# VectorE's small steps moved to PSUM, ScalarE and GpSimd, one lo piece, and one scale per weight matrix

## The chip, the core and the metric

The kernel runs on one NeuronCore of a Trainium2 chip. Its time is the device time of one execution in microseconds (us), the median of several runs. The engines are TensorE (PE, matmuls; PEld loads its weights), VectorE (DVE), ScalarE (ACT), GpSimd (POOL) and SyncE (SP), which only issues DMAs. [...]

## The reference

An attention over 8 batches, 12 heads, 448 tokens and head size 64 is followed by a layer that mixes each token with the one before it:

```python
q_n, k_n = rmsnorm(q, g_q), rmsnorm(k, g_k)        # x / sqrt(mean(x*x) + 1e-6) * g
scores = q_n @ k_n.T / 8; attn = softmax(scores)
x = (attn @ v)                                      # heads joined: 8 x 448 x 768
x_prev = x shifted by one token (zero in front)
xk = mu_k * x + (1 - mu_k) * x_prev
xr = mu_r * x + (1 - mu_r) * x_prev
k = relu(xk @ w_k)                                  # 768 x 1024
out = sigmoid(xr @ w_r) * ((k * k) @ w_v)           # 768 x 768, 1024 x 768
```

All inputs are fp32 apart from the three weight matrices, which arrive as 64-bit floats; the kernel reads each of their values as two 32-bit words and makes fp32 of them.

## The kernel before, in words

All products that matter are computed to about fp32 from fp16: each operand is split into hi (its fp16 value) and lo (the rest, again fp16), and a product is three matmuls, hi x hi, hi x lo and lo x hi. The first three of 24 quads (a quad is four heads of a batch, so three quads are a batch) use fp32 operands instead.

**Attention.** `stats` squares a quad's q and k (ScalarE), folds the halves (GpSimd), sums (VectorE) and takes the inverse root of 28 numbers per partition in `rsqrt`: two steps that make a first guess and three Newton rounds of three VectorE steps. With the two steps that scale and add epsilon that is 13 small VectorE steps, all on SBUF tiles (sst, stm, ss). `preps` scales q and k and splits and transposes them. `scores` computes a group, 128 query rows of two heads against 448 keys, in two PSUM banks; there are seven groups in a quad, 168 in all. `expo` takes the row maximum (VectorE, tile sums) and the exponential (ScalarE, in place in PSUM). In `split` ScalarE writes hi, scaled by 1 / sum, to SBUF (tile nat), and VectorE writes lo in two pieces of 64 and 384 columns (lines 889 and 890), so that lo's 64-token blocks stand rotated by one; a DMA transpose on SP's queue turns hi and lo for the second product. `attends` multiplies with v; `PASSES` lists which block goes with which block of v.

**v.** `vload` brings one pair of heads into one of two vf tiles, `vprep` squares it for a bound, takes a power of two as its scale (tile bstat), writes hi (ScalarE, vh) and lo (VectorE, vl). `batch_scales` works out a batch's scales (tile bsc, VectorE).

**Mixture.** `mix` (lines 952 to 967), twelve times per batch (six d for xk and six for xr): GpSimd multiplies the shifted x into df, VectorE adds the product of x to it, ScalarE writes hi, GpSimd lo.

**Weights.** w_k, w_r and w_v are cut in 20 tiles of 128 columns (8, 6 and 6; 768 or 1024 values per partition). `wload` loads each in two halves, issued on ScalarE's queue; `weights` turns each half from 64-bit words to fp32 in a wf tile: GpSimd the low part, ScalarE the top part into a PSUM bank of the `mm` share, VectorE joins the two. `wsplit` (1014 to 1038) then takes for each tile a scale from the diagonal of its Gram product (a TensorE product, VectorE's dg, a product with ones, VectorE's maximum, two small VectorE steps on WSC) and splits the tile into hi and lo (`wkh`, `wkl` and so on): tiles 1 to 13 on GpSimd with a ScalarE copy, the others on ScalarE and VectorE.

**Second layer.** `moe` runs batch by batch: eight products for k (144 matmuls), then, after `until(lambda: st["wdone"] == NW)` in the first batch, products of 128 tokens with w_r and w_v (294 matmuls per batch on average), each in a PSUM bank of the `mm` share. `gate` runs three tanh per 384 columns, one per weight tile, `store` multiplies, and GpSimd scales 384 columns before the output DMA on SP.

**What sets the order.** Every step is a Python generator that yields instructions; `Plan.run` emits, engine by engine, the instruction that could start first by the kernel's own price list (`price`), less 0.1 ns per unit of its thread's priority. The order on each engine and DMA queue is fixed when the program is built, and semaphores alone keep it at run time. The weights' priority is

```python
PRIO_W + (BOOST_W if st["want"] == "w" else 0) + (plan.now() - W_START - W_GAP * st["wdone"]) * W_PUSH
```

with W_GAP = 10e3 ns: it rises with time and falls by one step with each tile that is done. PSUM banks are lent by shares: `Share(psum, most, spare)` gives at most `most` banks and only while more than `spare` are free: scores (5, 1), second layer (2, 0), values and others (2, 0). A score group asks for two free banks, three in the first quads.

Since one helper records all instructions, every row of the profile has line 273; the tile names tell the steps apart (a name with x at its end is the same kind of tile added late).

Of the kernel before, what the change touches and what calls it, by code (L numbers as in the profile page):

```python
# [31 lines left out]
WF_BUFS = 2  # L32
# [6 lines left out]
LOW_TILES = range(0, 20)  # L39
POOL_TILES = range(1, 14)  # L40
# [36 lines left out]
Q_DVE = 1  # L77
PE_T = 6
# [10 lines left out]
WB_A = 'ot'  # L89
WB_B = 'mm'  # L90
# [5 lines left out]
W_GAP = 10e3  # L96
# [7 lines left out]
LATE_BUFS = (("kf", 1), ("df", 1), ("nat", 1))  # L104
# [65 lines left out]

def price(op):
# [4 lines left out]
    ps = any(in_psum(x) for x in aa)  # L176
    if e == "DVE":
        two = "in1" in kw
        c = n / 0.96 + (128 if two and n > 64 else 64)
        return c, c + 80  # L180
    if e == "ACT":
        c = n * 0.868 + (127 if ps else 67)
        if kw.get("accum_out") is not None:
            return c + 52, c + 170
        return c, c + 110
    if op.fn.__name__ == "memset":
        return 50, 95
    if "in1" in kw:
        c = n * (2.15 if kw["out"].dtype == F16 else 2.0) + 40
    elif n < 100:  # L190
        c = n * 0.868 + 180
    else:
        c = n * 1.27 + 35
    return c, c + 45

# [10 lines left out]
class Plan:  # L206
# [60 lines left out]
    def emit(self, ops):  # L267
# [18 lines left out]
        elif ops[0].fn.__name__.startswith("dma"):  # L286
# [3 lines left out]
            if "transpose" in op.fn.__name__:  # L290
                w, iss, tot = n / 128 * 1.21, 1600, 4000
            else:
                w, iss, tot = n / 55, 640, 3300
# [12 lines left out]
        else:  # L306
# [7 lines left out]
            if e == "POOL" or e == "DVE" and not any(in_psum(x) for x in op.kw.values() if isinstance(x, bass.AP)) and width(op.kw["out"]) > 2:  # L314
# [126 lines left out]
def attn_moe_kernel(tc, q, k, v, g_q, g_k, mu_k, mu_r, w_k, w_v, w_r, out):  # L441
# [15 lines left out]
    banks = {n: Share(psum, *c) for n, c in (("sc", SC_SHARE), ("mm", MM_SHARE), ("ot", OT_SHARE))}  # L457
# [18 lines left out]
    for nm, kt, n in (("wk", ND, D_FF), ("wr", ND, D_MODEL), ("wv", NF, D_MODEL)):  # L476
        WS[nm] = (wpool.tile([P, kt, n], F16, name=nm + "h"), wpool.tile([P, kt, n], F16, name=nm + "l"))
    pairs = [(b, hp) for b in range(B) for hp in range(NP)]
    quads = [(b, j) for b in range(B) for j in range(NP // 2)]
    NQ, NPAIR, NSS, NSL = len(quads), len(pairs), 4 * NT, (NT + 1) // 2  # L480
    VFREE = [const.tile([P, 2 * NSL, HD], F32, name="vf%d" % n) for n in range(VF_BUFS)]
# [5 lines left out]

    def WB(ci):
        return WB_A if ci < NF else WB_B

# [9 lines left out]
    def late():  # L500
# [11 lines left out]
        "vh": Ring(ap_, [P, 2 * NSL, HD], F16, "vh", VH_BUFS, plan),  # L512
# [9 lines left out]
        "raw": Ring(stage, [P, NF // 2, 2 * P], I32, "raw", RAW_BUFS, plan),  # L522
# [4 lines left out]
    for name, plan_ in (("kk", KK_LENT), ("xk", XK_LENT)):  # L527
# [5 lines left out]
        for n in plan_:  # L533
# [10 lines left out]
            if len(r.shape) == 3:  # L544
# [27 lines left out]
    def mu_stats():  # L572
        yield from until(lambda: st["lu"] >= 1 and len(WFT))
# [34 lines left out]
    def stats():  # L608
        for u in range(NQ):
# [4 lines left out]
            tm = small.tile([P, NSS], F32, name="stm", bufs=3)  # L614
# [11 lines left out]
            yield V.tensor_scalar(out=ss[:, 0:2 * NT], in0=ss[:, 0:2 * NT], scalar1=1.0 / HD, scalar2=1e-6, op0=ALU.mult, op1=ALU.add)  # L626
            yield V.tensor_scalar(out=ss[:, 2 * NT:NSS], in0=ss[:, 2 * NT:NSS], scalar1=gm[:, 3:4], scalar2=gm[:, 4:5], op0=ALU.mult, op1=ALU.add)
            yield from rsqrt(V, y, ss, tm, NEWTON_ON == "POOL" and G_)
# [69 lines left out]
    def vload():  # L698
        yield from until(lambda: st.get("vf") and st.get("lu", 0) >= LEAD_V)
        for i in range(NPAIR):  # L700
# [3 lines left out]
            yield SP.dma_start(out=vf.rearrange("p a c -> p (a c)"), in_=v[i])  # L704
# [15 lines left out]
    def vprep(js):  # L720
# [7 lines left out]
        for e, i in enumerate(js):  # L728
            yield from until(lambda: i in VF and st["tq"] >= GATE_V)
            vf = VF.pop(i)  # L730
            if half:
                vh = yield from R["vh"].get()
                vl = yield from R["vl"].get()
                sq = vh.bitcast(BF16)
# [4 lines left out]
            yield A.activation(out=sq, in_=vf, func=AF.Square, accum_out=vs[:, e:e + 1])  # L739
# [7 lines left out]
        yield V.tensor_reduce(out=vs[:, 2:2 + n], in_=pt[:, 0:n * P].rearrange("p (a c) -> p a c", c=P), axis=AX.X, op=ALU.max)  # L747
        banks["ot"].put(pt)
        sv, iv = s_[:, hp:hp + n], s_[:, NP + hp:NP + hp + n]
        yield V.tensor_scalar(out=sv.bitcast(I32), in0=vs[:, 2:2 + n].bitcast(I32), scalar1=24, scalar2=23, op0=ALU.logical_shift_right, op1=ALU.logical_shift_left)  # L750
# [487 lines left out]
```

## Time and profile before

| | |
|---|---|
| runs (us) | 1014.79, 1018.15, 1019.3; median 1018.15 |
| the profiled execution | 1015.21 us, of which span 1013.4 |
| mean granted TensorE clock | 0.961 of full speed |
| busy, share of the span | PE 926.0 (91%), DVE 812.7 (80%), ACT 746.0 (74%), POOL 691.8 (68%) |
| HBM read / written | 51.98 MB / 11.01 MB |
| DMA, mean over the span | 146 GB/s |

Matmuls overlap in the records, so 91% for PE is the time in which at least one of them was in flight. A row of the groups reads: line, engine, operation, out<-in by tile names, shapes, count | busy us, mean ns of one | idle time of the engine in front of them and what ended it. A row of the waits reads: who waited <- for what: us in total, times, longest.

### The profile page before, as it was taken

The page shows a single profiled execution, that of the slowest core. Times are in us where ns is not written, and L with a number is a line of the kernel's source. Part 1 is how long each engine was busy: PE and PEld are TensorE (multiplying, and loading weights), DVE is VectorE, ACT ScalarE, POOL GpSimd, SP SyncE. Part 2 cuts the span into 40 slices and gives each one's busy share as a digit, 9 for nine tenths or more (in the row PEclk, how much of TensorE's full clock was granted, in tenths as well). Part 3 has the DMA queues.
Part 4 walks back from the last instruction along what each step waited for, and adds up shares of the span by engine and source line. Part 5 has one row for each costly group of instructions (what it writes and reads, how often), then busy time and mean ns, then how long its engine had stood idle before and what let it go on. Part 6 is the DMA issues. An engine that isn't in the chain of part 4 may idle for free. (4 is left out here: it accounts for less than half of the span.)

```text
span 1013.4 us, 18593 instructions
## 1 busy us (share of the span) xinstructions
PE 926.0 (91%) x6082; PEld 485.8 (48%) x6082; DVE 812.7 (80%) x2260; ACT 746.0 (74%) x1756; POOL 691.8 (68%) x734
## 2 busy tenths in 40 slices
PE   2588869669999999999999999899999999999998
PEld 2354434335544555455545555355545454455564
DVE  5879998999998698979997998799997989763000
ACT  3667878878788789888887887878886988952311
POOL 2787889743798747877886859855987478556501
PEclk9878979869999999999999999999999999999999
DMA  7322349667788789569847977869858884640000
GB/s 248 119 80 86 118 120 221 170 166 169 172 165 168 143 197 203 133 152 201 207 105 173 214 158 161 161 131 201 175 126 177 186 183 110 146 107 32 1 32 32
DMA packets 371138, 148.17 MB, mean 146 GB/s; under 512 B 338272, under 2 KB 355168, under 8 KB 371040
## 3 DMA queue, kind: packets, MB, share of 16 engines
q1 hardware_dynamic: 351792, 129.20, 57.0%
q10 hardware_dynamic: 19248, 17.77, 5.9%
q8 instruction: 48, 0.79, 0.3%
q14 instruction: 50, 0.41, 0.1%
HBM read 51.98 MB, written 11.01 MB: 62 GB/s over the span
## 5 line engine op out<-in xcount | busy, mean ns | idle before, releaser
L273 PE MATMUL ps<-wvh,kk 128*128 128x384 f16 x896 | 233.1, 326 | 0.8 <-DVE nat L273 0.8
L273 ACT ACTIVATE ps<-ps,sums 128x448 f32<-128x448 f32 x294 | 181.9, 621 | 52.5 <-DVE sums L273 48.9
L273 PE MATMUL ps<-xk,wkh 128*128 128x448 f16 x768 | 210.5, 356 | 4.8 <-DVE wf L273 3.9
L273 DVE SCALAR_TENSOR_TENSOR nat<-ps,sums,nat 128x64 f16<-128x64 f32 x480 | 190.7, 439 | 19.2 <-ACT nat L273 17.8
L273 DVE TENSOR_REDUCE sums<-ps 128x1 f32<-128x448 f32 x336 | 193.7, 612 | 15.4 <-PE ps L273 15.1
L273 PE MATMUL ps<-wrh,xr 128*128 128x384 f16 x672 | 179.9, 331 | 2.1 <-DVE nat L273 2.0
L273 ACT ACTIVATE nat<-ps,sums 128x448 f16<-128x448 f32 (+1 forms) x272 | 167.8, 659 | 16.9 <-DVE sums L273 7.1
L273 PEld LDWEIGHTS <-kk 128*128 128x128 f16 (+1 forms) x1362 | 129.2, 98 | 98.7 <-issue 13.5
L273 PE MATMUL ps<-stk 64*128 64x448 f16 (+3 forms) x1104 | 134.2, 390 | 26.4 <-ACT xk L273 6.2
L273 PE MATMUL ps<-wvl,kk 128*128 128x384 f16 x448 | 146.0, 326 | 0.0
L273 PE MATMUL ps<-xk,wkl 128*128 128x448 f16 x384 | 136.5, 355 | 0.0
L273 PEld LDWEIGHTS <-xr 128*128 128x128 f16 x1008 | 96.4, 99 | 80.1 <-issue 16.9
L273 PE MATMUL ps<-wrl,xr 128*128 128x384 f16 x336 | 111.1, 331 | 0.0
L273 PEld LDWEIGHTS <-wkh 128*128 128x128 f16 x768 | 71.9, 99 | 81.6 <-issue 21.6
L273 POOL TENSOR_TENSOR o<-o,bsc 128x384 f32<-128x384 f32 x48 | 43.3, 902 | 88.3 <-DVE o L273 52.3
L273 DVE SCALAR_TENSOR_TENSOR o<-o,ps 128x384 f32<-128x384 f32 x56 | 30.5, 545 | 87.7 <-PE ps L273 59.2
L273 PE MATMUL ps<-pT,vh 128*64 128x448 f16 x588 | 93.8, 363 | 1.4 <-DMA pT<-nat 0.7
L273 ACT ACTIVATE o<-ps,bsc 128x128 f32<-128x128 f32 x144 | 45.6, 387 | 51.2 <-PE ps L273 33.1
L273 POOL TENSOR_TENSOR qk<-qk,ss 128x896 f32<-128x896 f32 x36 | 64.0, 1778 | 22.1 <-DVE ss L273 14.9
L273 PEld LDWEIGHTS <-stk 64*128 64x128 f16 x1008 | 35.0, 98 | 78.0 <-issue 35.5
L273 DVE SCALAR_TENSOR_TENSOR df<-x,bsc,df 128x448 f32<-128x448 f32 x68 | 61.0, 910 | 5.8 <-POOL df L273 5.7
L273 POOL TENSOR_TENSOR nat<-nat 128x448 f32<-128x448 f32 x41 | 48.2, 1175 | 23.6 <-ACT nat L273 17.1
(161 smaller groups left out, 1813.7 us busy)
## 6 DMA issues: line engine op xcount, KB each, us to landing
vf<-in_v_dram SPq DMA_DIRECT2D x48, 256.0 KB, 3.0
out_dram<-o SPq DMA_DIRECT2D x28, 384.0 KB, 2.7
qk<-in_k_dram SPq DMA_DIRECT2D x23, 448.0 KB, 4.4
qk<-in_q_dram SPq DMA_DIRECT2D x22, 448.0 KB, 4.3
raw<-in_moe_w_v_dram ACTq DMA_DIRECT2D x12, 512.0 KB, 4.2
raw<-in_moe_w_r_dram ACTq DMA_DIRECT2D x12, 384.0 KB, 3.3
kk<-in_moe_w_k_dram ACTq DMA_DIRECT2D x8, 384.0 KB, 3.9
raw<-in_moe_w_k_dram ACTq DMA_DIRECT2D x8, 384.0 KB, 3.7
```

The costliest lines, as they stand in the source:

```text
L273: r = op.fn(op.kw["out"], op.kw["value"]) if op.fn.__name__ == "memset" else op.fn(**op.kw)
```

## The change

- `stats`, `rsqrt`: the sums of squares are scaled into a PSUM bank (new share `df`), and all root steps but the last output work there.
- `split`: lo is written in one piece of 448 columns, not rotated; instead the host lays v's blocks out a second time shifted by one (`NVB` = 14 blocks for 8), vload, vf and vh get longer, and `PASSES` takes the shifted blocks.
- `vprep`: v's scale steps work in PSUM; v is scaled by GpSimd, hi is a ScalarE copy, lo a GpSimd subtraction.
- `batch_scales`, `outscale`: small VectorE steps go to GpSimd.
- `mix`: the product of the shifted x is made by ScalarE into a PSUM bank of the share `df`, which VectorE reads.
- Weights: the host lays each half tile out in one run per partition; the loads are issued by SP. A tile is converted into the next tile's slot of the split weights (which holds hi and lo of a tile in one place), the last into a wf tile (one buffer, two before). The Gram products of all tiles of a matrix add up in one PSUM bank (share `pg`), conversions use a share `wz` of two banks; one scale per matrix is taken after its last tile, and then all its tiles are split one after the other, even tiles on GpSimd, odd ones on ScalarE and VectorE.
- `gate`, `store`: with one scale, one tanh per 384 columns, and one GpSimd scaling of 768.
- W_GAP is 7e3 for 10e3, the price list is replaced, the late pool gives no third df buffer.

```diff
-WF_BUFS = 2
+WF_BUFS = 1
-LOW_TILES = range(0, 20)
-POOL_TILES = range(1, 14)
+WZ_SHARE = (2, 0)
+PG_SHARE = (1, 0)
+DF_SHARE = (2, 1)
+POOL_TILES = range(0, 20, 2)
-W_GAP = 10e3
+W_GAP = 7e3
-LATE_BUFS = (("kf", 1), ("df", 1), ("nat", 1))
+LATE_BUFS = (("kf", 1), ("nat", 1))
...
+            qs = yield from banks["df"].get()
+            sm, tm = qs[:, 0:NSS], qs[:, NSS:2 * NSS]
+            yield V.tensor_scalar(out=sm[:, 0:2 * NT], in0=ss[:, 0:2 * NT], scalar1=1.0 / HD, scalar2=1e-6, op0=ALU.mult, op1=ALU.add)
...
+            yield from rsqrt(V, y, sm, tm)
+            banks["df"].put(qs)
...
-            yield A.activation(out=vh, in_=vf, func=AF.Copy, scale=sv)
-            yield V.scalar_tensor_tensor(out=vl, in0=vf, scalar=sv, in1=vh, op0=ALU.mult, op1=ALU.subtract)
+                yield G_.tensor_scalar(out=vf, in0=vf, scalar1=sv, scalar2=0.0, op0=ALU.mult, op1=ALU.add)
+                yield A.copy(out=vh, in_=vf)
+                yield G_.tensor_tensor(out=vl, in0=vf[:, 0:2 * NSL], in1=vh[:, 0:2 * NSL], op=ALU.subtract)
...
-        for a, n, o in ((S - HD, HD, S), (0, S - HD, S + HD)):
-            yield V.scalar_tensor_tensor(out=ph[:, j, o:o + n], in0=sp[:, a:a + n], scalar=r[:, j:j + 1], in1=ph[:, j, a:a + n], op0=ALU.mult, op1=ALU.subtract)
+        yield V.scalar_tensor_tensor(out=ph[:, j, S:2 * S], in0=sp[:, 0:S], scalar=r[:, j:j + 1], in1=ph[:, j, 0:S], op0=ALU.mult, op1=ALU.subtract)
...
-        yield G_.tensor_scalar(out=df, in0=xp, scalar1=sc[:, j + ND:j + ND + 1], scalar2=0.0, op0=ALU.mult, op1=ALU.add)
-        yield V.scalar_tensor_tensor(out=df, in0=xc, scalar=sc[:, j:j + 1], in1=df, op0=ALU.mult, op1=ALU.add)
+        pb = yield from banks["df"].get()
+        yield A.activation(out=pb[:, 0:S], in_=xp, func=AF.Copy, scale=sc[:, j + ND:j + ND + 1])
+        yield V.scalar_tensor_tensor(out=df, in0=xc, scalar=sc[:, j:j + 1], in1=pb[:, 0:S], op0=ALU.mult, op1=ALU.add)
+        banks["df"].put(pb)
...
-                yield A.dma_start(out=raw[:, 0:hk, :], in_=w[i * P:(i + hk) * P, c * P:(c + 1) * P].bitcast(I32).rearrange("(i p) n -> p i n", p=P))
+                yield SP.dma_start(out=raw[:, 0:2 * hk * P], in_=w[c, h].bitcast(I32))
...
+            yield [T.matmul(form=("w", 110 * kt), out=pg[:, c % nb * P:(c % nb + 1) * P], lhsT=w16[:, i, :], rhs=w16[:, i, :], start=(c == 0 and i == 0), stop=(last and i == kt - 1)) for i in range(kt)]
+            if last:
+                plan.spawn(wscale(nm, kt, ci - c, ci + 1, pg, nb * P), wprio)
...
+        for ci in range(c0, c1):
+            plan.spawn(wsplit(nm, kt, ci - c0, ci, ci + 1 == c1), wprio)
...
-        for c in range(3):
-            m = 3 * h + c
-            yield A.activation(out=th[:, c * P:(c + 1) * P], in_=zr[:, c * P:(c + 1) * P], func=AF.Tanh, scale=rsu[:, m:m + 1])
+        yield A.activation(out=th, in_=zr[:, 0:NH], func=AF.Tanh, scale=rsu[:, 0:1])
...
-        yield G_.tensor_tensor(
-            out=th.rearrange("p (c n) -> p c n", n=P), in0=th.rearrange("p (c n) -> p c n", n=P),
-            in1=spread(rsu[:, ND + 3 * h:ND + 3 * h + 3], P), op=ALU.mult)
+            yield G_.tensor_scalar(out=o, in0=o, scalar1=rsu[:, 1:2], scalar2=0.0, op0=ALU.mult, op1=ALU.add)
```

More of the change, by code (lines that the diff above doesn't have):

```diff
@@ L77 @@
 Q_DVE = 1
+V_POOL = True
 PE_T = 6
@@ L88 @@
 SLACK_F = 6
-WB_A = 'ot'
-WB_B = 'mm'
 LEAD_V = 1
@@ L313, in emit @@
                 self.acc = acc
-            if e == "POOL" or e == "DVE" and not any(in_psum(x) for x in op.kw.values() if isinstance(x, bass.AP)) and width(op.kw["out"]) > 2:
+            if e in self.held and shares(op):
                 for a, b in self.held["DVE" if e == "POOL" else "POOL"]:
@@ L572, in mu_stats @@
     def mu_stats():
-        yield from until(lambda: st["lu"] >= 1 and len(WFT))
+        yield from until(lambda: st["lu"] >= 1 and len(RAW))
         yield A.dma_start(out=mu[:, 0, 0, :], in_=mu_k.rearrange("(t p) -> p t", p=P))
@@ new lines, in weights @@
+            if c == 0:
+                pg = yield from banks["pg"].get()
+            last = ci + 1 in (NF, NF + ND, NW)
+            nb = 2 if ci < NF else 1
+            if last:
+                wf = yield from R["wf"].get(ci < NF)
+                f = wf.rearrange("p i n -> p (i n)")[:, 0:kt * P]
+                WFT[nm] = wf
+            else:
+                f = WS[nm][:, c + 1].rearrange("p a i n -> p (a i n)").bitcast(F32)
+            fi = f.bitcast(I32)
+            for h in range(2):
+                yield from until(lambda: (ci, h) in RAW and st["tq"] >= GATE_W)
+                raw = RAW.pop((ci, h))
+                n = kt * P // 2
+                cols = slice(h * n, (h + 1) * n)
+                zb = yield from banks["wz"].get()
+                z = zb[:, 0:n]
+                yield G_.tensor_scalar(out=fi[:, cols], in0=raw.bitcast(mybir.dt.uint8)[:, 0:8 * n].rearrange("p (n b) -> p n b", b=8)[:, :, 3], scalar1=-15.5, scalar2=2.0 ** -5, op0=ALU.add, op1=ALU.mult)
+                yield A.activation(out=z, in_=raw[:, 0:2 * n].rearrange("p (n two) -> p n two", two=2)[:, :, 1].bitcast(F32), func=AF.Prelu, scale=F64_EXP, alpha=F64_NEG)
+                yield V.scalar_tensor_tensor(out=fi[:, cols], in0=z.bitcast(I32), scalar=3, in1=fi[:, cols], op0=ALU.logical_shift_left, op1=ALU.bitwise_or)
+                banks["wz"].put(zb)
@@ L1037, in wsplit @@
-        R["wf"].put(WFT.pop(ci))
+            yield A.copy(out=hi, in_=f)
+            yield G_.tensor_tensor(out=lo, in0=f, in1=hi, op=ALU.subtract)
+        else:
+            yield A.activation(out=hi, in_=f, func=AF.Copy, scale=sc)
+            yield V.scalar_tensor_tensor(out=lo, in0=f, scalar=sc, in1=hi, op0=ALU.mult, op1=ALU.subtract)
+        if last:
+            R["wf"].put(WFT.pop(nm))
         st["wdone"] += 1
```

190 lines of the change are left out of this document (93 added, 97 removed).

## The prediction

> **What bounds the kernel now.** First the table of stretches (busy us and count of PE, PEld, VectorE (DVE), ScalarE (ACT), GpSimd (POOL); then granted clock, DMA share, GB/s), cut where the products with the last weights begin, which the next three rows date (each with its first and last start).
>
> ```profile
> 0.00:40.00 40.00, 12.89 (x59) 8.78 (x60) 26.62 (x84) 16.23 (x31) 15.30 (x21) 0.91 0.56 185
> 40.00:227.50 187.50, 147.11 (x877) 78.46 (x876) 167.74 (x462) 145.91 (x328) 149.77 (x177) 0.84 0.53 140
> 227.50:880.00 652.50, 637.34 (x4355) 325.36 (x4356) 582.36 (x1635) 541.05 (x1291) 477.39 (x479) 0.99 0.76 166
> 880.00:1013.40 133.40, 128.63 (x795) 73.20 (x793) 35.93 (x82) 42.79 (x109) 49.39 (x59) 1.00 0.16 46
> ```
> ```profile
> L273 PE MATMUL ps<-wrh,xr x672: 325/326/528, 227.5 to 1004.4; 128*128 128x384 f16 x168
> ```
> ```profile
> L273 ACT CAST wrh<-wf x6: 814/832/834, 113.0 to 164.6; 128x768 f16<-128x768 f32 x6
> ```
> ```profile
> L273 ACT ACTIVATE wvh<-wf,WSC x6: 1133/1149/1165, 176.3 to 226.1; 128x1024 f16<-128x1024 f32 x6
> ```
>
> In the first table, from 227.5 on, TensorE is the bound: 637.3 of 652.5 us, a matmul per 150 ns (652.5 / 4355), the clock at 0.99. Before 227.5 it isn't: 936 matmuls in 227.5 us, which at 150 ns would be 140 us (an estimate, the mix differs). So some 87 us of TensorE's time are lost in the first stage, 56 of them after 40 us, where VectorE is the fullest engine: 167.7 of 187.5 us, 89%. ScalarE has 78%, GpSimd 80%. TensorE's largest engine wait there is for VectorE's weight step:
>
> ```profile
> PE ps L273 <- DVE wf L273: 12.3, 9, 3.9
> ```
>
> The first stage ends with the weights: the planner holds the second product back until all 20 column tiles are split, and wv's six splits start 10 us apart ((226.1 - 176.3) / 5), wr's 10.3. That is the planner's constant of 10 us per tile, not an engine's speed. So two things can shorten this stage, a lighter fullest engine and a quicker pace; behind it only TensorE's idle 15.2 us are to be had.
>
> **VectorE in the first stage (40 to 227.5).**
>
> ```profile
> L273 DVE SCALAR_TENSOR_TENSOR nat<-ps,sums,nat 128x384 f16<-128x384 f32 x28 | 16.9, 604 | 0.0
> L273 DVE SCALAR_TENSOR_TENSOR df<-x,bsc,df 128x448 f32<-128x448 f32 x12 | 10.7, 908 | 0.0
> L273 DVE SCALAR_TENSOR_TENSOR wvl<-wf,WSC,wvh 128x1024 f16<-128x1024 f32 x6 | 9.2, 1541 | 0.4 <-ACT wvh L273 0.4
> ...
> L273 DVE SCALAR_TENSOR_TENSOR nat<-ps,sums,nat 128x64 f16<-128x64 f32 x28 | 7.7, 274 | 1.2 <-ACT nat L273 1.0
> ...
> L273 DVE TENSOR_SCALAR WSC<-WSC 128x1 int32<-128x1 int32 x36 | 5.2, 144 | 0.2
> L273 DVE TENSOR_REDUCE WSC<-ps 128x1 f32<-128x128 f32 x18 | 5.1, 284 | 2.6 <-PE ps L273 2.5
> L273 DVE SCALAR_TENSOR_TENSOR stm<-stm,ss 128x28 f32<-128x28 f32 x12 | 5.1, 421 | 0.2
> L273 DVE SCALAR_TENSOR_TENSOR vl<-vf,bstat,vh 128x512 f16<-128x512 f32 x5 | 5.0, 1007 | 0.0
> L273 DVE TENSOR_TENSOR dg<-ps,ident 128x128 f32<-128x128 f32 x18 | 5.0, 279 | 0.8 <-PE ps L273 0.8
> L273 DVE SCALAR_TENSOR_TENSOR ss<-stm,ss 128x28 f32<-128x28 f32 x12 | 4.9, 412 | 0.2
> L273 DVE TENSOR_TENSOR stm<-sst,ss 128x28 f32<-128x28 f32 x12 | 3.2, 268 | 0.2
> ...
> L273 DVE TENSOR_SCALAR sums<-ps 128x2 f32<-128x2 f32 x15 | 2.2, 149 | 1.7 <-ACT ps L273 1.7
> ```
>
> The two lo pieces give 1.03 ns per element ((604 - 274) / 320), so one of 448 costs 604 + 66 = 670 ns in place of 878: 28 x 208 = 5.8 us. The mixture gets one operand from PSUM, as the lo piece has: 670 for 908, 12 times, 2.9 us. v's subtraction leaves: 5.0. The scale: 15.3 us (5.2 + 5.1 + 5.0) for 18 tiles become three rounds, double width at most, some 1.3 us each: 11.4. The root's 36 Newton steps average 367 ns on SBUF operands; in PSUM no row has 28 columns, and the nearest, 149 ns for two, gives 149 + 27 = 176: 13.2 - 6.3 = 6.9 (at worst nothing, if the steps wait for each other). Back come weight splits, ten odd tiles for six: with 768 columns at three quarters of 1541, 7 x 1.16 + 3 x 1.54 = 12.7 for 9.2, or 3.5 more. Sum: 32.0 - 3.5 = 28.5 off, VectorE falls from 167.7 to 139. The four small steps of each root and the batch scales are left uncounted, a few us more.
>
> [...]
>
> **What the other engines take on there.**
>
> ```profile
> L273 ACT ACTIVATE ps<-raw 128x512 f32<-128x512 f32 x12 | 7.7, 638 | 1.3 <-DVE wf L273 0.9 <-DVE WSC L273 0.3
> ```
> ```profile
> L273 ACT ACTIVATE vh<-vf,bstat 128x512 f16<-128x512 f32 x5 | 3.7, 732 | 0.0
> ```
> ```profile
> L273 ACT ACTIVATE x<-ps 128x448 f32<-128x448 f32 x3 | 1.6, 535 | 0.4 <-PE ps L273 0.4
> ```
> ```profile
> L273 ACT ACTIVATE x<-ps,bstat 128x448 f32<-128x448 f32 x2 | 1.3, 648 | 0.0
> ```
> ```profile
> L273 ACTq DMA_DIRECT2D raw<-in_moe_w_r_dram x12: 374/374/393, 80.6 to 144.9; - x12
> L273 ACTq DMA_DIRECT2D raw<-in_moe_w_v_dram x12: 374/374/375, 155.0 to 211.0; - x12
> ```
> ```profile
> L273 POOL TENSOR_SCALAR wf<-wf,WSC 128x768 f32<-128x768 f32 x11 | 11.0, 999 | 1.9 <-DVE WSC L273 0.7 <-PE ps L273 0.6
> ...
> L273 POOL TENSOR_TENSOR wrl<-wf,wrh 128x768 f16<-128x768 f32 x6 | 9.8, 1641 | 1.5 <-ACT wrh L273 1.4
> L273 POOL TENSOR_SCALAR df<-x,bsc 128x448 f32<-128x448 f32 x12 | 8.4, 710 | 1.1 <-DVE bsc L273 1.0
> ```
>
> ScalarE: x's product into PSUM costs between 535 (no scale from memory) and 700 (638 plus the 113 that such a scale adds, less 64 columns): 12 x 0.65 = 7.8 us. v's copy goes from 512 to 896 columns, no more than 0.4 us each, 2 us. Against that, 24 issues of weight loads at 374 ns, 9 us, go to SP's queue. What comes out is 146 + 10 = 156 of busy time, with the issues gone. The mixture's product adds a wait: it needs a PSUM bank that VectorE has finished reading. Behind it in ScalarE's queue stand the exponentials, for which VectorE's lo steps and in the end TensorE wait; a bank is back after one VectorE step, so I price this wait inside the fill of the engines below. SP, which sets these loads among its transposes and waits in order for a free raw buffer, delays what is queued behind it; no row prices that, between nothing and a landing of 4 us now and then. I take it as hidden, since TensorE doesn't use SP's transposes in the first three quads.
>
> GpSimd: loses 12 x 0.71 = 8.5; gets v five times. By its split rows (1.3 ns per element scaling, 2.1 subtracting) that is 5 x (1.17 + 1.09) = 11.3. It splits 10 tiles for 13: at 2.64 per narrow and 3.5 per wide tile, 7 x 2.64 + 3 x 3.5 = 29 for 34. Small scales, at most 3. Net about nothing: 150.
> [...]
>
> **The sum.** At the same work the fullest engine falls from 168 to 156, and it is another one. At 89% fill that is a stage of 175 us, at 95% of 164: 12 to 23 us less; the upper half because three engines would be almost level (156, 150, 139), which a planner fills better than one full one, the lower because the chains between them stay as long. The pace adds to it: 7 us per tile for 10 would put the last split up to 20 x 3 = 60 us earlier. Most of that isn't time won: the attention steps that the weights then pass are done later, on the same engines, and TensorE needs their products. And wv's six splits can start only when its last half tile is converted, three of them in a row on GpSimd, 3 x 3.5 = 10.5 us, where now one split of 1.15 + 1.54 us follows the last tile: some 8 us back. Between nothing and 45 us I take 9 net for the pace, near the low end because the work is moved and not removed. First stage: 18 + 9 = 27 us, with bounds of 5 and 55.
>
> Later VectorE loses as well:
>
> ```profile
> L273 DVE TENSOR_REDUCE sums<-ps 128x1 f32<-128x448 f32 x252 | 144.9, 612 | 6.8 <-PE ps L273 6.6
> ```
> ```profile
> L273 DVE SCALAR_TENSOR_TENSOR nat<-ps,sums,nat 128x64 f16<-128x64 f32 x203 | 55.7, 274 | 18.0 <-ACT nat L273 16.8 <-POOL natx L273 1.1
> ```
> ```profile
> L273 DVE SCALAR_TENSOR_TENSOR vl<-vf,bstat,vh 128x512 f16<-128x512 f32 x36 | 38.9, 1080 | 10.9 <-ACT vh L273 10.7
> ```
>
> the second lo piece keeps only its 64 columns (203 x 0.066 = 13), so at least 42 + 39 of VectorE's 582 us go. But ScalarE gets up to 84 mixtures (96 in all less the 12 above), 84 x 0.65 = 55 on 541, and takes VectorE's place at 91%; that one wide tanh replaces three is left uncounted on the other side. A helper at nine tenths stays beside TensorE, only another one. Of TensorE's idle 15.2 us I take 4 (0 to 10). Longer v blocks bring 42 x 192 KB = 8.1 MB, at the rate of the weights' queue
>
> ```profile
> q10 hardware_dynamic: 19248, 17.77, 5.9%
> ```
>
> (17.77 MB in 60 us) some 27 us of the 16 engines in 652, beside a share of 0.76: hidden. 17 fewer f32 products lie where TensorE waits anyway: nothing. At the end GpSimd scales 768 columns at once where
>
> ```profile
> 1009.37 0.83 POOL L273 TENSOR_TENSOR o<-o,bsc 128x384 f32<-128x384 f32 x1 [5.90 <-DVE o L273]
> ```
>
> stands; 999 ns for 830: 0.2 us more. The profiled execution took 1015.2 us, its span of 1013.4 and 1.8 around it that stay: 1015.2 - 27 - 4 + 0.2 = 984. The median of the runs, 1018.15, is 0.3% above the profiled one, so 987.
>
> **Rivals.** *The pace decides.* The 10 us spacing is so exact that only the constant can set it. If the last split moves 45 us forward, and little attention is put off, with 5 us later on: 968. Against it: TensorE needs the put-off work anyway.
>
> *The stage doesn't shrink.* The moves don't do what they say: steps with a PSUM operand keep their length (then VectorE loses 28.5 - 9.8 = 19), and GpSimd's subtraction of v costs what its row of 768 columns does (1641), 5 x 0.55 = 2.8 us more, which makes it as full as ScalarE; the whole-matrix scale takes back its 8 us. Of the 18 us from fill half remain, of the pace nothing: 1018 - 9 + 2 = 1011, within 1004 to 1020. For it: GpSimd is already at 80%; against it: the lo rows, which have a PSUM operand and are the cheapest per column.
>
> *PSUM banks run out: slower.* Of eight banks products may hold 2, values 2 and now mixture and root 2, in the first stage weights 3 more; a score group needs two free and one spare. If mixture, values and products hold five, one group at a time is in flight. 252 reduces behind 227.5 are 126 groups, one per 5.2 us (652.5 / 126). The last batch's 438 products take 71 us (at 162 ns, 128.63 / 795), so attention may end 58 us later than 880 unharmed. With the 31 us gained, the kernel gets slower if a group takes over 5.2 + (58 + 31) / 126 = 5.9 us; at 6.1 it loses 0.2 x 126 = 25 us and ends near 1043. For it: all three queues can be full at once. Against it: values and mixtures hold banks only for a few us each.
>
> **How the numbers follow.** Forecast 0.45 (975 to 1003), pace decides 0.20, stage doesn't shrink 0.20 (0.12 faster, 0.08 within), banks 0.15. A measurement here tells 0.5% (5 us) from no change. Faster: 0.45 + 0.20 + 0.12 = 0.77; same 0.08; slower 0.15. The range, 962 to 1018, leaves out the banks case and the far end of the pace.
>
> **What would show it.** The first product with wr starts between 175 and 205 instead of 227.5; VectorE's share before it falls below 82%; one lo step of about 670 ns, a mixture step of 670, root steps below 200; ScalarE becomes the fullest helper at about 90%; TensorE stays above 96% behind that. It is wrong if wr's first product stays beyond 215, or if TensorE falls below 92% in the middle, with score products waiting for a bank.

## The result, and the profile after

The changed kernel takes 1002.38 us (median of 4 runs, 1001.81 to 1002.68), the kernel before 1017.42 beside it: a ratio of 0.9857, with a 95 % interval of 0.9836 to 0.9877. Forecast were 987 us. The sign was right, and the time lies inside the range, but the gain is 15.0 us by these medians, 12.5 us by the profiled spans (1013.4 to 1000.9), where 31 were worked out.

The table of stretches of the changed kernel, cut at 40 us and where its products with wr begin and where its last score reduce ends (a score reduce is VectorE's row maximum for 128 query rows of one head, 336 in all; columns as in the prediction):

```profile
0.00:40.00 40.00, 9.84 (x45) 6.13 (x46) 22.71 (x78) 13.15 (x26) 9.77 (x17) 0.98 0.51 172
40.00:206.20 166.20, 129.87 (x787) 68.01 (x786) 135.64 (x338) 138.21 (x306) 139.37 (x168) 0.86 0.53 145
206.20:843.00 636.80, 618.47 (x4312) 317.61 (x4310) 484.65 (x1360) 582.50 (x1323) 470.83 (x495) 0.99 0.93 190
843.00:1000.90 157.90, 152.91 (x911) 86.72 (x909) 20.66 (x43) 47.37 (x88) 55.91 (x66) 1.00 0.10 28
```

The first stage (what lies before the first product with wr) ends 21 us earlier, at 206.2 for 227.5. In it no helper is filled as VectorE was before (89 %): they stand at 82, 83 and 84 %. Behind it ScalarE has VectorE's place, 91.5 %, and the DMA engines' share is 0.93 for 0.76. But the earlier end holds less work: 832 matmuls lie before it (45 + 787), 936 before. So the two kernels are compared at one time, 320 us, by what they have left. First the kernel before, then the changed one:

```profile
0.00:320.00 320.00, 251.64 (x1550) 134.05 (x1551) 284.69 (x795) 238.62 (x543) 229.68 (x261) 0.89 0.61 152
320.00:1013.40 693.40, 674.33 (x4534) 351.76 (x4531) 527.96 (x1466) 507.37 (x1214) 462.17 (x474) 1.00 0.65 144
```
```profile
0.00:320.00 320.00, 248.46 (x1580) 130.26 (x1582) 244.20 (x655) 254.23 (x564) 235.59 (x273) 0.93 0.66 164
320.00:1000.90 680.90, 662.62 (x4471) 348.21 (x4470) 419.47 (x1162) 526.99 (x1177) 440.30 (x471) 0.99 0.74 153
```

At 320 us the changed kernel has 4471 matmuls left for 4534, at some 150 ns each 9.5 us less: that is what was gained by then, in and just behind the first stage. It does the rest at 152.3 ns per matmul (680.9 / 4471) for 152.9, another 3 us. The forecast had 27 and 4.

The single prices are not where it went. The steps that the change reshapes, by form, over the whole changed kernel:

```profile
L289 DVE SCALAR_TENSOR_TENSOR nat<-ps,sums,nat 128x448 f16<-128x448 f32 x242 | 158.7, 677 | 56.3 <-ACT nat L289 55.8
L289 ACT ACTIVATE ps<-x,bsc 128x448 f32<-128x448 f32 x96 | 64.4, 683 | 0.8 <-DVE nat L289 0.7
L289 DVE SCALAR_TENSOR_TENSOR df<-x,bsc,ps 128x448 f32<-128x448 f32 x96 | 63.8, 674 | 54.1 <-ACT ps L289 46.6 <-POOL xr L289 6.9 <-POOL vf L289 0.2
L289 POOL TENSOR_TENSOR vl<-vf,vh 128x512 f16<-128x512 f32 x42 | 48.8, 1161 | 10.6 <-ACT vh L289 10.5
```

677 ns for 670 forecast, 683 for 650, 674 for 670, 1161 for 1090. VectorE's idle time in front of its lo and mixture steps, 56.3 and 54.1 us, now mostly ends with ScalarE (55.8 and 46.6 us): VectorE waits for ScalarE.

### The profile page after: what moved, and what is told of

It is laid out like the page before. It is cut to its first block, busy times and chain, and to the rows that moved or that the text cites. A ratio compares the mean times of both kernels' runs of the same rounds, so it can differ in the third digit from the quotient of the medians.

```text
span 1000.9 us, 18138 instructions
## 1 busy us (share of the span) xinstructions
PE 911.1 (91%) x6048; PEld 478.5 (48%) x6048; DVE 663.7 (66%) x1816; ACT 781.2 (78%) x1740; POOL 675.9 (68%) x744
## 5 line engine op out<-in xcount | busy, mean ns | idle before, releaser
L289 PE MATMUL ps<-wv,kk 128*128 128x384 f16 x1344 | 233.8, 326 | 1.4 <-DVE df L289 1.4
L289 PE MATMUL ps<-xk,wk 128*128 128x448 f16 x1152 | 226.1, 353 | 2.8 <-DVE nat L289 2.2
L289 ACT ACTIVATE ps<-ps,sums 128x448 f32<-128x448 f32 x294 | 189.3, 646 | 18.3 <-DVE sums L289 16.7
L289 DVE SCALAR_TENSOR_TENSOR nat<-ps,sums,nat 128x448 f16<-128x448 f32 x242 | 158.7, 677 | 56.3 <-ACT nat L289 55.8
L289 PE MATMUL ps<-wr,xr 128*128 128x384 f16 x1008 | 180.3, 330 | 2.4 <-DVE o L289 1.3
L289 PEld LDWEIGHTS <-wk 128*128 128x128 f16 (+1 forms) x1194 | 113.4, 99 | 113.5 <-issue 14.2
L289 DVE SCALAR_TENSOR_TENSOR df<-x,bsc,ps 128x448 f32<-128x448 f32 x96 | 63.8, 674 | 54.1 <-ACT ps L289 46.6
L289 ACT ACTIVATE o<-ps,bsc 128x384 f32<-128x384 f32 x48 | 28.9, 603 | 76.5 <-PE ps L289 76.5
L289 ACT ACTIVATE ps<-x,bsc 128x448 f32<-128x448 f32 x96 | 64.4, 683 | 0.8 <-DVE nat L289 0.7
L289 POOL TENSOR_TENSOR xr<-df,xr 128x448 f16<-128x448 f32 x48 | 49.5, 1042 | 21.8 <-ACT xr L289 21.7
L289 POOL TENSOR_SCALAR vf<-vf,bstat 128x896 f32<-128x896 f32 x42 | 42.8, 1019 | 28.2 <-DVE bstat L289 16.3
```

What stands on the lines that cost most here:

```text
L289: r = op.fn(op.kw["out"], op.kw["value"]) if op.fn.__name__ == "memset" else op.fn(**op.kw)
```

## The experiments

Ratios are to the kernel before, run on the same chip, with the 95 % interval in brackets; the changed kernel has 0.9857. "Left at 320" is the count of matmuls after 320 us, taken from each trace as above but with the kernel's total less the count before 320 (so 4532 for the kernel before, 4468 for the changed one). The expectations count TensorE's lost time at 320 us instead; 1 us of it is some 6.7 matmuls left, at 150 ns each.

**How much the order alone is worth.** Five kernels differ from one of the two only in a factor of the planner on the helpers' durations, 1.0 in both; the instructions are the same, and the planner writes them in another order. ctl (changed kernel), b_s1002 and b_s0998 (kernel before), a_s0998 and a_s1004 (changed):

```
-OP_SLOW = 1.0
+OP_SLOW = 1.002
```

> Changed kernel with the planner's factor for the durations of the three helpers at 1.002 for 1.0: not one instruction more or less, only the order in which the planner writes them can differ. Theory E (a good part of what single edits gave here, such as 1.7 us more with a wait removed, is the order that the planner happens to find): the time moves by 3 to 10 us either way. Rival: it stays within 2 us, and the differences of 6 us and more that single edits gave are their own.

> Kernel before with the planner's factor for helper durations at 1.002: the same instructions, another order, as the control on the changed kernel that brought 1 % (ratio 0.9764 for 0.9857). Theory E (the order that the planner happens to find is worth some 10 us either way in both kernels, and the change's 1.4 % is one draw against one draw): 0.990 to 1.012, off 1.000 by more than 0.3 %. Rival (the kernel before sits in a settled order and only the changed one is open): within 0.3 % of 1.000.

> Kernel before with the same factor at 0.998, a third order of the same instructions. Theory E: again between 0.990 and 1.012 and not the value of the other two; the mean of the three orders stays above the mean of the changed kernel's by 1 to 2.5 %, if the change has a gain of its own. Rival F (no gain of its own): the best of the three reaches 0.985, the changed kernel's time.

> Changed kernel with the factor at 0.998. Theory E: between 0.974 and 0.998, off 0.9857 by more than 0.3 %. If the change has a gain of its own of about 15 us, all its orders stay below 0.995. Rival F: this order lies at 0.995 or above, among those of the kernel before.

> Changed kernel with the factor at 1.004, a fourth order. Theory E: between 0.974 and 0.998, and by the trace the difference to the other orders comes after 250 us, in single waits of TensorE at the change from one batch's products to the next, each 1 to 8 us with the lower clock behind it, and not in the first stage, where the order with 1.002 lost the same as that with 1.0 (99 to 100 us at 240). Rival (the first stage decides): the difference is there by 240 us.

| kernel | ratio | first wr product, us | left at 320 | span, us |
|---|---|---|---|---|
| before | 1 | 227.5 | 4532 | 1013.4 |
| b_s1002 | 1.0116 (1.0094 to 1.0137) | 231.9 | 4576 | 1023.5 |
| b_s0998 | 1.0029 (1.0015 to 1.0043) | 233.7 | 4575 | 1017.1 |
| changed | 0.9857 (0.9836 to 0.9877) | 206.2 | 4468 | 1000.9 |
| ctl | 0.9764 (0.9739 to 0.9789) | 207.4 | 4471 | 991.4 |
| a_s0998 | 0.9889 (0.9854 to 0.9924) | 208.4 | 4508 | 1004.4 |
| a_s1004 | 0.9853 (0.9830 to 0.9876) | 210.6 | 4462 | 998.0 |

A factor that changes no instruction moves the time by up to 1.2 %. So one pair of kernels is one draw against one draw. The three orders of the kernel before have a mean of 1.005, the four of the changed kernel 0.984: some 2.1 %, and all four lie below all three, so the change has a gain of its own (rival F falls). Its size is known to about 1 % either way, an estimate from the scatter of these seven ratios. By the spans it is 19.3 us (1018.0 less 998.7). At 320 us the means are 4561 and 4477 matmuls left, 84 fewer or 12.6 us at 150 ns; the other 6.7 us come behind.

Where ctl differs from the changed kernel shows what an order is worth. At 320 us they have 4471 and 4468 left; the 9.5 us between their spans come later, in single waits. (The first stage can differ by order too: in the kernel before 44 matmuls more are left with 1.002, in the changed kernel 40 more in a_s0998.) One of them in the changed kernel, TensorE's timeline (start and length in us; in brackets the idle time before and what ended it), at the change from batch 4's products with wk to those with wr (batches counted from 0):

```profile
653.81 0.76 PE L289 MATMUL ps<-stk 64*64 64x448 f16 x12
654.50 1.31 PE L289 MATMUL ps<-xk,wk 128*128 128x448 f16 x6
659.55 1.30 PE L289 MATMUL ps<-stk 64*128 64x448 f16 x6 [3.74 <-DVE nat L289]
660.79 4.09 PE L289 MATMUL ps<-wr,xr 128*128 128x384 f16 x18
```

and ctl at the same place:

```profile
645.96 0.74 PE L289 MATMUL ps<-stk 64*128 64x448 f16 x6
647.01 3.09 PE L289 MATMUL ps<-wr,xr 128*128 128x384 f16 x18 [0.31 <-ACT kf L289]
650.15 3.09 PE L289 MATMUL ps<-wv,kk 128*128 128x384 f16 x18
```

In the one, score products placed ahead of the wr products wait 3.74 us for a VectorE step on nat and hold everything behind them; in the other the wr products come at once. Here the wait costs twice: the 18 wr matmuls after it take 4.09 us for 3.09. The granted clock was lower there, 0.86 from 660 to 670, where ctl has 1.00 (640 to 660). The changed kernel from 650 on in steps of 10 us:

```profile
650.00:660.00 10.00, 5.66 (x40) 2.52 (x39) 6.48 (x16) 10.00 (x23) 8.29 (x7) 0.97 1.06 202
660.00:670.00 10.00, 10.00 (x64) 4.92 (x60) 7.25 (x23) 8.05 (x20) 7.33 (x10) 0.86 0.85 178
670.00:680.00 10.00, 10.00 (x78) 5.33 (x78) 8.44 (x28) 9.53 (x23) 6.40 (x9) 1.00 0.85 143
```

**The pace.** gap10 is the changed kernel with the old constant, b_gap7 the kernel before with the new one:

```
-W_GAP = 7e3
+W_GAP = 10e3
```

> Changed kernel with the planner's constant at 10 us per weight tile, as before the change; everything else stays. The forecast put 9 us of the gain down to the pace. Rival B (the pace sets the stage): the first product with wr goes back from 206 to about 222 to 228, and the time rises by 9 us or more, to a ratio of 0.995 or higher. Theory A (the pace only reorders work that the same three helpers have to do, weights first and the first batch's attention later): wr's first product starts up to 10 us later, the products of batch 0 with wk up to 10 us earlier, and the time stays within 4 us of the changed kernel, a ratio between 0.982 and 0.990.

> Kernel before with one constant changed: 7 us per weight tile for 10. In the changed kernel putting this constant back to 10 cost 1.9 % (ratio 1.0045 for 0.9857), more than the whole gain. Theory P (the pace alone carries the gain: the weights' steps and the small steps that follow them get their place in the queues earlier): the kernel before gets 8 to 16 us faster by it, ratio 0.984 to 0.992, and its first product with wr starts by 210. Theory Q (the two need each other: an earlier pace takes engine time that VectorE, at 89 % in the first stage, doesn't have before the change): the ratio stays between 0.995 and 1.010, the first wr product moves less than 10 us, and the attention of batch 1 (its last score reduce at 246.7) ends over 8 us later.

gap10: 1.0045 (1.0030 to 1.0061), the whole gain and more; wr's first product at 241.2, later than before the change. b_gap7: 1.0137 (1.0109 to 1.0164), though wr's first product comes at 216.8 for 227.5: by 320 us it has 4532 matmuls left, exactly as many as with 10 us, the end of batch 1's score reduces moves from 246.7 to 255.3, and the rest takes 155.1 ns per matmul for 153.0 ((1023.0 - 320) / 4532). Nearest is theory Q, though the time lies above its 1.010 and wr's first product moves 10.7 us where it allowed 10: in this one order an earlier pace with the old work buys nothing.

What 10 us does to the changed kernel is seen in the small steps behind the last split. VectorE and GpSimd in gap10, first those of VectorE:

```profile
218.11 1.13 DVE L289 TENSOR_SCALAR WIN<-WSC 128x12 int32<-128x12 int32 x1
226.47 0.22 DVE L289 TENSOR_SCALAR WIN<-WIN,smu 128x6 f32<-128x6 f32 x1
226.70 0.22 DVE L289 TENSOR_SCALAR WIN<-WIN,wsc 128x6 f32<-128x6 f32 x1
232.58 0.92 DVE L289 TENSOR_SCALAR WIN<-WIN,wsc 128x6 f32<-128x6 f32 x1
```
```profile
234.44 0.27 POOL L289 TENSOR_SCALAR bsc<-WIN,bsc 128x1 f32<-128x1 f32 x1
...
240.68 0.18 POOL L289 COPY carry<-bsc 64x2 f32<-64x2 f32 x1
```

Some 3.5 us of work are stretched over 22, because the constant sets the due time by which the planner ranks these steps among the attention's. The first wr product waits for them in the planner's order. In the changed kernel itself the same steps are stretched as well, over 17 us (185.1 to 202.3, wr's first product at 206.2), but its last split ends 33 us earlier, at 185.1. tail10 and tail10_s1002 keep 10 us and give these steps a rank of their own:

```
-        return PRIO_W + (BOOST_W if st["want"] == "w" else 0) + (plan.now() - W_START - W_GAP * st["wdone"]) * W_PUSH
+        return PRIO_W + (BOOST_W if st["want"] == "w" else 0) + (plan.now() - W_START - W_GAP * st["wdone"]) * W_PUSH + (2000 if st["wdone"] == NW else 0)
...
-            plan.spawn(outscale(b), PRIO_O)
+            plan.spawn(outscale(b), PRIO_O if b else 2000)
```

> Changed kernel with 10 us per weight tile, and the small steps behind the last split (four of VectorE on the inverse scales, then four of GpSimd) put ahead of everything else by a priority of their own. With 10 us alone they were stretched over 22 us, from 218.1 to 240.7, and the first product with wr followed at 241.2, though the products with wk were done at 206.7 and the attention of batch 1 at 234.7 for 246.3. Theory T (the constant acts through the planner's due times of that tail, not through the splits themselves): wr's first product at 218 to 224 and the time 12 to 20 us less than with 10 us alone, a ratio of 0.985 to 0.993; the lighter engines are then worth 8 to 15 us by themselves. Rival P (the early splits themselves carry it): the first wr product moves by less than 8 us and the ratio stays above 1.0.

> The changed kernel with 10 us per weight tile and the small steps behind the last split put first, in the order that the factor 1.002 gives. Theory T (once that tail comes first the pace has no effect): the first product with wr between 208 and 222, lost time at 320 us 105 to 114, and a ratio of 0.974 to 0.990, the spread of the changed kernel's orders. Rival P (the pace has a part of its own): above 0.990. If it comes out below 0.976 it is the fastest of all.

tail10: 0.9878 (0.9854 to 0.9902); tail10_s1002: 0.9864 (0.9850 to 0.9879). In tail10 the same steps of VectorE run from 218.1 to 219, and the wr products begin at 215.9. So 10 us with these steps (the tail) in their place is worth the same as 7 us without that rank: theory T holds in its times, though tail10's wr products begin earlier than its 218 to 224, and no gain from the pace as such is seen. The two together, 7 us and the rank, were not run. This pair also shows the lighter engines alone. Before the change 74 score reduces are done when wr's first product starts, in all three orders, at 227.5 to 233.7; tail10 has 74 at 215.9, tail10_s1002 72 at 221.3. At equal attention that is about 12 us (231.0 less 218.6 in the means, 11.6 for the two profiles with the planner's factor at 1.0). The row of tail10 for this stage (columns as before):

```profile
40.00:215.90 175.90, 134.61 (x850) 71.17 (x850) 146.88 (x369) 152.52 (x344) 144.18 (x169) 0.87 0.60 161
```

**Which engine sets the first stage.** dvep, actp and poolp add steps that nobody needs to one helper each, behind each of the 40 half-tile conversions. actp (dvep has three steps on VectorE, poolp one on GpSimd in this place):

```
+    junk = const.tile([P, 96], F32, name="junk")
...
+                for _ in range(2):
+                    yield A.activation(out=junk, in_=junk, func=AF.Copy, scale=1.0)
```

> The same with two steps of 96 columns on ScalarE behind each half-tile conversion, some 0.3 us, 12 us in all. Theory H with ScalarE as the engine (the forecast had it fullest): TensorE's lost time at 320 us rises by 9 to 12 above 107 to 114, ratio 0.994 to 1.000. Theory G: a rise by 2 to 6, as with the other two.

> Changed kernel with work added that does nothing: behind each of the 40 half-tile conversions three steps of 96 columns on a scratch tile on VectorE, some 0.3 us each time, 12 us in all, none of it awaited by another engine. In the first stage VectorE then goes from 82 to about 85 %. Theory G (chains between three level helpers set the stage, no single engine does): TensorE's lost time at 320 us, 107 to 114 in four orders, rises by 2 to 6, and about as much as with the same load on the other two. Theory H (one engine sets it): with the load on that engine it rises by 9 to 12, with it on the other two by less than 2. By the forecast's own reading (ScalarE fullest) VectorE's load is free: ratio within 0.976 to 0.989, the spread of the orders.

> The same with one step of 96 columns on GpSimd, about 0.3 us, 12 us in all. In the changed kernel's first stage GpSimd is the fullest by a little, 84 %, for 82 and 83 %. Theory H with GpSimd as the engine: lost time at 320 us rises by 9 to 12, ratio 0.994 to 1.000. Theory G: a rise by 2 to 6, as with the other two.

The loads came out larger than planned. By form, from the three traces in the order of their names (dvep, actp, poolp):

```profile
L289 DVE TENSOR_SCALAR junk<-junk 128x96 f32<-128x96 f32 x120 | 48.4, 404 | 0.9
```
```profile
L289 ACT ACTIVATE junk<-junk 128x96 f32<-128x96 f32 x80 | 23.1, 289 | 0.4
```
```profile
L289 POOL TENSOR_SCALAR junk<-junk 128x96 f32<-128x96 f32 x40 | 14.5, 362 | 0.6
```

These are sums of spans, and the spans of neighbouring steps overlap in the records. Over the whole kernel the busy time rises by 37.7 us on VectorE (663.7 to 701.4), by 12.8 on ScalarE (781.2 to 794.0) and by 11.0 on GpSimd (675.9 to 686.9).

ScalarE's load costs nothing: 4464 matmuls are left at 320 for 4468, the ratio is 0.9885 (0.9870 to 0.9899), wr's first product comes at 206.3, though ScalarE is now busy 148.0 of the 166.2 us before it, 89 % for 83 %:

```profile
40.00:206.20 166.20, 128.86 (x777) 69.00 (x778) 136.43 (x335) 148.02 (x370) 137.97 (x164) 0.85 0.53 143
```

GpSimd's load costs 84 matmuls (4552), 12.6 us, ratio 0.9992 (0.9978 to 1.0006). VectorE's costs 154 matmuls (4622), 23 us, ratio 1.0116 (1.0096 to 1.0136). Both are beyond the 46 matmuls that the orders of the changed kernel lie apart. So ScalarE, which the forecast had as the new fullest engine, doesn't set the stage. A load on VectorE or on GpSimd does cost time there, so theory G, which had all three alike, falls, and theory H, which had one engine alone, isn't met either. In poolp the added steps themselves end only one wait of TensorE's weight loads, of 0.7 us; but TensorE's waits for GpSimd's nat steps between 40 and 320 us rise from 9.4 to 18.0 us. In dvep the two engines aren't separate: 75 of the 120 added steps run beside a GpSimd instruction and take 523 ns on average, the other 45 take 204.

The test of the other sign moves ten weight scalings from GpSimd to ScalarE (wact, and wact_s1002 in the second order):

```
-            yield G_.tensor_scalar(out=f, in0=f, scalar1=sc, scalar2=0.0, op0=ALU.mult, op1=ALU.add)
+            yield A.activation(out=f, in_=f, func=AF.Copy, scale=sc)
```

> Changed kernel with one step of ten weight tiles moved from GpSimd to ScalarE: the scaling of the f32 tile in place, 0.9 to 1.0 us each, so some 10 us off GpSimd and 9 onto ScalarE in the first stage. Theory H with GpSimd (its load came through at 12 of 13.4 us, ScalarE's at 0 of 19.2): TensorE's lost time at 320 us falls from 107 to 98 to 101 and the ratio from 0.986 to about 0.978, give or take the spread of orders (0.6 %). Rival (the forecast's reading, ScalarE fullest; or chains, to which the place of a step is nothing): lost time at 320 us stays at 106 to 114, ratio 0.985 or above.

> The same in the order that the factor 1.002 gives, where the changed kernel had the ratio 0.9764 and 107.6 us of lost time at 320 us. Theory H with GpSimd: 98 to 102 at 320 us, ratio about 0.969, and with it the fastest of all kernels here. Rival: 106 to 114, ratio 0.976 to 0.990.

A miss. GpSimd falls from 139.4 us between 40 and 206 to 128.4, the fifth pair in wact's row (after PE, PEld, DVE and ACT):

```profile
40.00:206.00 166.00, 129.57 (x755) 67.66 (x755) 135.66 (x350) 145.46 (x313) 128.38 (x159) 0.83 0.53 151
```

Yet wact's first wr product comes later, at 217.5, and 4477 and 4513 matmuls are left at 320 for 4468 and 4471; the ratios are 0.9898 (0.9876 to 0.9919) and 1.0042 (1.0027 to 1.0057). wact_s1002 has its first wr product at 200.4, 7 us earlier than ctl, and loses it behind: between 266 and 280 TensorE stands 9.2 us in four waits (vact, below, shows what is going on there). A load put on GpSimd costs, the same load taken off doesn't pay: GpSimd alone doesn't set the stage either. What does, beyond "not ScalarE", stays open.

**Parts undone one at a time.** mixpool puts the mixture's first product back on GpSimd and into SBUF, vact v's scale and lo part on ScalarE and VectorE (V_POOL = False), mu the old gate of the mu loads, shortv cuts the loads of v:

```
-        pb = yield from banks["df"].get()
-        yield A.activation(out=pb[:, 0:S], in_=xp, func=AF.Copy, scale=sc[:, j + ND:j + ND + 1])
...
+        yield G_.tensor_scalar(out=df, in0=xp, scalar1=sc[:, j + ND:j + ND + 1], scalar2=0.0, op0=ALU.mult, op1=ALU.add)
```
```
-V_POOL = True
+V_POOL = False
```
```
-        yield from until(lambda: st["lu"] >= 1 and len(RAW))
+        yield from until(lambda: st["lu"] >= 1 and st.get("cv"))
...
+            st["cv"] = True
```
```
-            w = (2 * NSL if i < 2 * U32 else NVB) * HD
+            w = 2 * NSL * HD
```

> Changed kernel with one part undone: the mixture's first product goes back from ScalarE and PSUM to GpSimd and SBUF, 96 of them (VectorE's mixture step then has two SBUF operands: about 900 ns for 674). Theory D (in the middle ScalarE, at 91.5 % busy, is the bound behind TensorE): ScalarE falls to about 82 % there, GpSimd rises from 74 to about 84 %, TensorE's idle time in the middle falls from 18 us by 5 to 10, and the kernel gets 4 to 9 us faster than the changed one unless the first stage loses it (there 8 us return to GpSimd, 3 to VectorE, and 8 leave ScalarE). Rival C (the DMA engines at 0.93 set the middle): ScalarE's share falls but TensorE's idle time stays at 18 us or rises. Theory A for the first stage: GpSimd, at 84 %, gets 8 us more, so wr's first product comes 3 to 8 us later.

> Changed kernel with one part undone: v is scaled on ScalarE and its lo part subtracted on VectorE, as before the change (the longer blocks stay). In the first stage GpSimd loses 5 x 2.2 = 11 us and VectorE gets 5 us. Theory A (three level helpers): the work goes from the fullest of them to the least full, so the stage shortens by 2 to 6 us; in the middle nothing changes, since VectorE has 24 % free there; ratio 0.980 to 0.985. Rival (VectorE is still the engine that the first stage waits for, since its queue is what TensorE waits for): the stage gets 3 to 5 us longer, ratio 0.989 or more. Theory D: ScalarE's step takes 1.1 us for 0.98, 42 times, 5 us more in the middle, which costs up to 5 us there.

> Changed kernel with one gate put back: the loads of the two mu vectors wait for the first converted weight tile again, so VectorE's step on them no longer stands in its queue at 13 us. Theory A (the first stage is now set by waits between three helpers that are level at 82 to 84 % busy, and VectorE's 5.2 us wait for mu between 13 and 18 us is one of them, which nothing makes up for): 3 to 6 us less than the changed kernel, so a ratio of about 0.981 to the kernel before, the first product with wr at about 201 us for 206. Rival B (the pace of 7 us per weight tile dates the end of the stage whatever happens at its start): the first product with wr stays within 1 us of 206 and the ratio at 0.986. Rival E (any edit makes the planner write another order, worth a few us either way): a change with no relation to that wait, the first wr product the same or later although the wait is gone.

> Changed kernel in which the loads of v bring only the first 512 of 896 columns, 256 KB for 448 KB, 42 times; the other columns hold zeros, so the product of the probabilities' lo part with v is left out of the result. All instructions stay. It prices the 8 MB more. Theory C (the DMA engines, at 0.93 in the middle for 0.76, hold the middle back): share back to about 0.88, landing times of the transposes shorter (4.2 us for 4.7), TensorE's idle time in the middle less by 5 us or more, ratio 0.975 to 0.981. Rival (hidden, as forecast): the ratio stays within 0.3 % of 0.9857. The planner counts these loads as shorter, so a change of some us by its order is possible either way.

| kernel | ratio | first wr product, us | left at 320 |
|---|---|---|---|
| mixpool | 1.0074 (1.0061 to 1.0088) | 217.2 | 4551 |
| vact | 0.9924 (0.9909 to 0.9940) | 197.5 | 4490 |
| mu | 0.9882 (0.9866 to 0.9898) | 206.3 | 4484 |
| shortv | 0.9910 (0.9885 to 0.9934) | 205.7 | 4498 |

mixpool is the only one well outside the orders' spread: 83 matmuls or 12.5 us more left at 320, and slower behind it as well. With this one product back on GpSimd the whole gain is gone (in this one order). The root in PSUM, the one lo piece and the scale per matrix were not undone one at a time, so what each of them brings stays open. Behind mixpool's first stage ScalarE falls to 84 %:

```profile
217.00:880.00 663.00, 640.56 (x4423) 328.50 (x4422) 515.12 (x1372) 559.45 (x1262) 548.33 (x585) 0.99 0.88 182
```

(559.45 of 663) and TensorE still idles 22.4 us, for 18.3 in the changed kernel's middle: theory D falls, a ScalarE at 91 % is not what holds TensorE there. In shortv the DMA share from 206 to 843 us goes from 0.93 to 0.87, TensorE idles 22.8 us, and the transposes land no sooner (4.7 us in both): theory C falls too, and nothing of the 8 MB more shows (the ratio is 0.5 % above the changed kernel's, more than the 0.3 % of the rival, but less than an order moves). mu misses: VectorE's wait of 5.2 us at 13 us is gone and nothing comes of it. vact lies 0.7 % above the changed kernel, less than the 1.2 % that an order moves, and meets neither of its theories. Its first wr product comes 8.7 us earlier, and TensorE then stands three times, 10.3 us in all, between 264 and 280. That stretch of vact:

```profile
260.00:285.00 25.00, 13.95 (x86) 5.70 (x85) 24.61 (x62) 24.47 (x57) 12.27 (x15) 0.66 1.09 234
```

Batch 0's products are done, batch 1's with wk begin only at 280.4, and what is left is the attention that was put off: VectorE and ScalarE are busy 98 % of the time with it, GpSimd half, and TensorE's clock is at 0.66. So in vact, and in wact_s1002, an earlier end of the first stage is paid back at the helpers' rate as soon as the products run out. No version with a cause that can be named beats the changed kernel; the fastest of all, ctl, is an order (992.93 us, 0.9764).

## Why the prediction was right in sign and wrong in size

**What bounds the kernel**: right as a description, incomplete as a bound. Most of the gain is made by 320 us (12.6 of 19.3 us in the means of the orders), and before wr's first product it is a load on VectorE or GpSimd, not on ScalarE, that costs time.

**The fill, 18 us forecast, about 12 measured** (tail10 at equal attention). The busy times were near: in tail10's stage ScalarE, GpSimd and VectorE have 152.5, 144.2 and 146.9 us where 156, 150 and 139 were worked out, though VectorE lost 21 us and not 28.5. The step that failed is the one from there to the stage's length, "At the same work the fullest engine falls from 168 to 156, and it is another one", with a fill of 89 to 95 %. ScalarE is the fullest, but the stage doesn't follow from its busy time: actp fills it to 89 % and loses nothing. And the three nearly level engines were not filled better than one full one: tail10's stage takes 175.9 us, with ScalarE at 87 %. That is the lower end of the 12 to 23 us, for which the chains between the engines were the stated reason; which chains these are stays open.

**The pace, 9 us forecast, nothing measured.** The step "Between nothing and 45 us I take 9 net for the pace" is the other half of the miss. The last split did end 44 us earlier, at 185.1 for 228.8, and the stage 21 us earlier, just outside the 175 to 205 that were to show it; but 104 fewer matmuls lay before it, and the work put off was paid back by 320 us. With 10 us and the tail put first the time is the same. What the forecast didn't see is that the constant also ranks the small steps behind the last split; low in rank they cost 17 us (gap10 against tail10), 13 of them by 320 us.

**The middle, 4 us forecast**: 3 in the profiled pair, 6.7 with the end in the mean of the orders. ScalarE at 91.5 % was forecast at 91, TensorE above 96 % came out at 97.1, and nothing of the longer v blocks shows. That the size fits is in part luck: the 4 us were to come out of TensorE's idle time in the middle, and in the two tables that rises from 15.2 to 18.3 us. From 320 us to the last score reduce it falls by 1 us in this pair (14.3 to 13.3), by 3 in the means of the orders (14.4 to 11.3).

**The root in PSUM (tile ps in the rows), 176 ns forecast, 180 to 193 measured in the first stage**, for 367 on SBUF. The price was near, but the forecast had no reason why the steps on SBUF were long. The two traces show that some were long and most were not, by minimum, median and maximum; first a step of the kernel before, then one of the changed kernel:

```profile
L273 DVE SCALAR_TENSOR_TENSOR stm<-stm,ss x72: 164/186/1511, 15.7 to 856.8; 128x28 f32<-128x28 f32 x72
```
```profile
L289 DVE SCALAR_TENSOR_TENSOR ps<-ps,ss x72: 171/195/196, 21.0 to 779.9; 128x28 f32<-128x28 f32 x72
```

The median hardly changes (186 on SBUF, 195 in PSUM: 9 ns more there); the long ones are gone. Sorted by whether a GpSimd instruction runs at the same time, the 28 steps stm<- of before between 40 and 227.5 us take 471 ns (16 with) and 183 ns (12 without), and the 16 steps ss<- of after 180 (12 with) and 184 (4 without). So beside a GpSimd instruction the steps on SBUF were 2.6 times as long on average, and those with an operand in PSUM were not longer; what holds up the former is not shown.

**The rivals.** The forecast's own case, 975 to 1003, holds the measured 1002.4 only at its edge. "The stage doesn't shrink" gave 1011 and was nearer in size (9 us off for 15) but not in mechanism: the PSUM steps became cheap (180 to 193 ns for 367), as forecast. PSUM banks did not run out: all 336 score reduces are done at 843 us for 894. "The pace decides" is refuted: the last split came 44 us earlier, and the time is far from its 968; tail10 does as well with the old pace.

**What the sum left out** is the order. It moves both kernels by up to 1.2 % and took some 7 us of the change's 19 in this pair of profiles (19.3 less 12.5). Even with these 7 us some 12 of the 31 are missing, 6 of the fill and 9 of the pace, less the 3 that came in addition behind 320 us.

## What to carry to other kernels

Where a planner writes the order, run two or three orders of each kernel before a difference of 1 % is given a cause, and compare the work left at one time, not the time of a landmark: a landmark can be moved by putting other work off. Busy time did not name the engine that sets the stage here (ScalarE at 89 % in actp, nothing lost); a useless load on each engine in turn tells more, if it is counted by the engine's total busy time, and a load taken away must confirm it. Small steps at the end of a chain need a rank of their own: here 3.5 us of them, ranked low, cost 17.

## What the runs showed of the hardware

In the changed kernel an idle time of TensorE cost more than itself: after 3.74 us the next 18 matmuls took 4.09 us for the 3.09 that they took in ctl, at a granted clock of 0.86 in those 10 us, where ctl had 1.00.

Three kinds of VectorE's steps on SBUF took longer on average while a GpSimd instruction ran. The 28 stm<- steps of the kernel before took 471 ns with one and 183 without. The 120 added steps of 96 columns in dvep had a median of 210 ns, a mean of 404 and a maximum of 1736; 523 on average beside a GpSimd instruction, 204 without. v's subtraction on VectorE had a median of 792 ns, a mean of 1064 and a maximum of 2252 (42 steps) and takes 1159 on GpSimd with little spread (1147 to 1184); 34 of VectorE's 42 ran beside a GpSimd instruction and took 1139 on average, the other 8 took 744 (732 to 752). The forecast used 1007 and 1080 as VectorE's price.
